# Rewriting an attention-plus-FFN training step in 512-token chunks

## Chip, cores and metric

The kernel runs on one core of a Trainium2 chip. The metric is the device time of one execution in microseconds (us), lower is better. Where a run differs by over 1.5% from the fastest of its kernel, it is called slow and left out of the ratios (medians are of all runs).

## The reference

One transformer layer, forward and backward, S = 2048 tokens, D = 512, 32 heads of 16, a hidden width of 1792, everything in bf16. Attention looks at 8 positions, 2 apart, backwards in time.

```python
x = A_x
h  = x + attention(layernorm(x)) @ wo      # W = 8 shifts, dilation 2, softmax over the 8
h2 = h + gelu(layernorm(h) @ w1 + b1) @ w2 + b2
# outputs: h2 and the gradients of x, wqkv, wo, w1, b1, w2, b2 for a given grad_out
idx = pos[:, None] - 2 * arange(8)[None, :]
logits = einsum("bhsd,bhswd->bhsw", q, k[idx]) * scale      # masked where idx < 0
o = einsum("bhsw,bhswd->bhsd", softmax(logits), v[idx])
```

On the chip a head group of 8 heads x 16 dims fills the 128 partitions. A weight per head has to stand on all 16 partitions of its head: that is the "broadcast". It is a DMA that reads 8 rows (one per head) 16 times each.

## The kernel before

It does each stage for all 2048 tokens: layernorm, QKV, logits, softmax, attention output, FFN, and backward in the reverse order. The parts that matter here:

```python
def bcast_rows_ap(d_tile, row0, col0, width):              # 8 rows, read 16 times
    base = d_tile[row0:row0 + 8, col0:col0 + width]
    rs = base.ap[-2][0]
    return _ap(base, [[0, DH], [rs, 8], [1, width]])

def a4_bcast(g):                                            # attention output, all tokens
    for w in range(W):
        if w % 3 == 1:
            pe_bcast(attnT_sb, g, w, bc, PADL, 0, S, ...)   # by matmul
        else:
            bq = [nc.sync, nc.scalar, nc.gpsimd][(g * W + w) % 3]
            bq.dma_start(out=bc[:], in_=bcast_rows_ap(attnT_d, 32 * w + 8 * g, PADL, S))
...
for g in range(G):
    bcs = bcs_next
    if g + 1 < G:
        bcs_next = a4_bcast(g + 1)                          # the next group's loads
    for w in range(W):
        nc.vector.tensor_tensor(out=prod[:], in0=bcs[w][:],
            in1=vT[:, g, PADL - DIL * w: PADL - DIL * w + S], op=ALU.mult)
        for c in range(NC):
            nc.tensor.matmul(accs[c][:], lhsT=ident[:], rhs=prod[:, c * 512:(c + 1) * 512], ...)
...
for ft in range(FT):                                        # gradient of w2
    transpose_T_to_tm(gT[:, ft:ft + 1, :], g_ft, 1)         # 16 TensorE transposes and evictions
    for t in range(NT):
        nc.tensor.matmul(ps[:], lhsT=g_ft[:, t, :], rhs=gout_bf[:, t, :], ...)
```

The store-and-load trip of the attention weights happens once for all tokens, and loads of the next group run under the products of this one.

## Time and profile before

| | us |
|---|---|
| time, median of 2 | 1067.77 (1067.63 to 1067.9) |
| TensorE / VectorE / ScalarE busy | 809 / 641 / 466 |
| forward ends at | about 384 |
| FFN backward with all gradients and the first attention-backward stages (384 to 812) | 428 |
| attention backward with its loads, LN backward and wqkv gradient (812 to 1065) | 253 |

Read it as a row of stages, each with its own bound; the lines stand in the prediction. No engine is full, so the time is made of the stages' bounds and the gaps between them.

### The profile page before, as it was taken

The numbers are of one execution on the slowest core, as the hardware profiler recorded it, in microseconds if no ns is written. First come the engines' busy times: TensorE is split into PE (matmuls) and PEld (weight loads), VectorE is DVE, ScalarE is ACT, GpSimd is POOL, SyncE is SP. The second block draws the span as 40 slices with busy tenths as digits, with TensorE's granted clock in tenths as the row PEclk, the third lists the DMA queues.
The fourth block names the chain that finished last, engine by engine and source line by source line (L and its number), as shares of the span: only waits on it lengthen the run. The fifth ranks groups of instructions, "written<-read, shape, count | busy, mean of one in ns | idle before, by whom it ended". The sixth has DMA issues, their size and how long they took to land.

```text
span 1065.2 us, 13636 instructions
## 1 busy us (share of the span) xinstructions
PE 809.0 (76%) x4993; PEld 395.8 (37%) x5066; DVE 640.6 (60%) x1317; ACT 465.7 (44%) x860; POOL 40.5 (4%) x70
## 2 busy tenths in 40 slices
PE   0894547874789968998652988744997899959898
PEld 0443312342334434443221444423544333324454
DVE  5309966781886614335994890697002999948822
ACT  3561153662997614445772223201643444432232
POOL 0000010000000000000000000000000011000000
PEclk9995558995999989999995998755998999979899
DMA  4231039317444450004552014201405999731100
GB/s 140 80 161 82 1 100 250 105 34 263 149 163 149 146 175 11 26 25 150 197 194 93 1 43 157 80 1 53 169 30 136 255 237 242 189 135 39 42 30 30
DMA packets 53990, 121.38 MB, mean 114 GB/s; under 512 B 5794, under 2 KB 22948, under 8 KB 53156
## 3 DMA queue, kind: packets, MB, share of 16 engines
q0 software_dynamic: 9968, 42.87, 12.8%
q1 hardware_dynamic: 25142, 41.30, 12.6%
q10 hardware_dynamic: 18814, 36.35, 10.9%
q8 instruction: 39, 0.64, 0.3%
q14 instruction: 27, 0.22, 0.1%
HBM read 81.01 MB, written 39.46 MB: 113 GB/s over the span
## 4 chain that ended last, share of the span: by engine, by line
PE 39%; DVE 19%; issue 18%; DMA 13%; ACT 8%; POOL 1%; SPq 1%; ACTq 0%; POOLq 0%; DVEq 0%
PE ps_gln L687 5%; PE pt L258 4%; PE ps_gw L804 4%; PE ps_gw L613 4%; PE ps_qkv L338 4%; PE ps_gwq L940 4%; DMA bc<-attnT_d 3%; PE ps_ffn L525 2%; DMA wqkv_nat<-in_A_wqkv_dram 2%; DMA bg<-glT_d 2%; DVE qg_row L654 2%; ACT x_row L544 2%; PE ps_h L541 2%; DVE qg_row L652 2%; ACT ch L547 2%
## 5 line engine op out<-in xcount | busy, mean ns | idle before, releaser
L854 DVE TENSOR_TENSOR prodv<-bv,grad_oT 128x1024 bf16<-128x1024 bf16 x64 | 39.6, 681 | 80.5 <-DMA bv<-attnT_d 80.4
L642 PE MATMUL ps_gg<-goutT,w2T 128*128 128x512 bf16 x218 | 52.2, 387 | 21.7 <-ACT gg L645 21.4
L613 PE MATMUL ps_gw<-gout_bf,g_ft 128*128 128x512 bf16 x216 | 63.2, 378 | 0.0
L541 PE MATMUL ps_h<-ln2T,w_bf 128*128 128x512 bf16 x217 | 52.9, 389 | 12.2 <-ACT x_row L544 11.8
L804 PE MATMUL ps_gw<-gh_tm,ln_re 128*128 128x512 bf16 (+1 forms) x248 | 57.3, 356 | 0.4 <-issue 0.2
L770 DVE TENSOR_TENSOR prod<-grad_oT,vT 128x1024 bf16<-128x1024 bf16 x64 | 38.9, 684 | 23.0 <-ACT grad_oT L145 22.3
L525 PE MATMUL ps_ffn<-w_bf,gT 128*128 128x512 bf16 x222 | 51.5, 379 | 0.9 <-ACT x_row L544 0.8
L246 PE MATMUL pt<-ident,ln_bf 128*128 128x128 bf16 x128 | 16.3, 274 | 47.1 <-DVE ln_bf L220 26.5
L438 DVE TENSOR_TENSOR prodo<-bc,qkvT 128x2048 bf16<-128x2048 bf16 x32 | 37.0, 1220 | 23.0 <-DMA bc<-attnT_d 19.2
L687 PE MATMUL ps_gln<-w1T,grad_h1T 128*128 128x512 bf16 x219 | 50.1, 381 | 0.2
L258 PE MATMUL pt<-ident,gT 128*128 128x128 bf16 x224 | 44.8, 217 | 6.1 <-ACT g_ft L145 2.3
L143 DVE COPY g_ft<-pt 128x128 bf16<-128x128 bf16 x112 | 25.1, 224 | 39.6 <-PE pt L258 39.6
L226 ACT ACTIVATE gy<-ps_gln 128x512 f32<-128x512 f32 x32 | 19.1, 597 | 66.7 <-PE ps_gln L687 35.3
L940 PE MATMUL ps_gwq<-gq_tm,ln_re 128*128 128x512 bf16 x185 | 47.7, 391 | 0.4 <-issue 0.2
L145 ACT COPY g_ft<-pt 128x128 bf16<-128x128 bf16 x112 | 29.9, 267 | 35.6 <-PE pt L258 35.6
L869 DVE TENSOR_TENSOR prodq<-bg,qkT 128x1024 bf16<-128x1024 bf16 x64 | 43.5, 680 | 2.6 <-DMA bg<-glT_d 2.6
L441 PE MATMUL acc_o<-prodo,ident 128*128 128x512 bf16 x125 | 37.9, 407 | 9.0 <-DVE prodo L438 8.0
L283 ACT CAST bg<-bp 128x512 bf16<-128x512 f32 (+1 forms) x72 | 28.6, 467 | 37.0 <-DVE prodk L872 15.0
L872 DVE TENSOR_TENSOR prodk<-bg,qkT 128x1024 bf16<-128x1024 bf16 x64 | 43.5, 679 | 0.1
L338 PE MATMUL ps_qkv<-ln1T,wqkv_p 128*128 128x512 bf16 x188 | 43.1, 384 | 0.2
L922 PE MATMUL ps_gln<-wqkvT,gqkvT 128*128 128x512 bf16 x187 | 42.9, 385 | 0.4 <-issue 0.2
L858 PE MATMUL accv<-prodv,ident 128*128 128x512 bf16 x124 | 37.9, 390 | 6.9 <-DVE prodv L854 6.5
(246 smaller groups left out, 1655.8 us busy)
## 6 DMA issues: line engine op xcount, KB each, us to landing
qg_row<-qg_d POOLq DMA_DIRECT2D x14, 512.0 KB, 3.7
sg_d<-sg SPq DMA_DIRECT2D x23, 256.0 KB
bv<-attnT_d SPq DMA_DIRECT2D x22, 256.0 KB
bv<-attnT_d ACTq DMA_DIRECT2D x22, 256.0 KB
bv<-attnT_d POOLq DMA_DIRECT2D x20, 256.0 KB, 6.2
qkvT_d<-qkvT ACTq DMA_DIRECT2D x2, 2080.0 KB
qkT<-qkvT_d POOLq DMA_DIRECT2D x2, 2080.0 KB, 13.6
bg<-glT_d ACTq DMA_DIRECT2D x16, 260.0 KB
```

Source lines behind the costliest of these rows:

```text
L258: nc.tensor.transpose(pt[:, j * P:(j + 1) * P], srcT[:, r, src_off + t * P: src_off + (t + 1) * P], idm_ap)
L338: nc.tensor.matmul(ps[:], lhsT=wqkv_p[:, dc, jt * P:(jt + 1) * P], rhs=ln1T[:, dc, c * 512:(c + 1) * 512], start=(dc == 0), stop=(dc == DC ...
L525: nc.tensor.matmul(ps[:], lhsT=gT[:, ft, t * P:(t + 1) * P], rhs=w2_bf[:, ft, :], start=(ft == 0), stop=False)
L541: nc.tensor.matmul(ps[:], lhsT=w1_bf[:, dc, ft * P:(ft + 1) * P], rhs=ln2T[:, dc, c * 512:(c + 1) * 512], start=(dc == 0), stop=(dc == DC ...
L613: nc.tensor.matmul(ps[:], lhsT=g_ft[:, t, :], rhs=gout_bf[:, t, :], start=(t == 0), stop=(t == NT - 1))
L642: nc.tensor.matmul(ps[:], lhsT=w2T[:, dc, ft * P:(ft + 1) * P], rhs=goutT[:, dc, c * 512:(c + 1) * 512], start=(dc == 0), stop=(dc == DC - 1))
L687: nc.tensor.matmul(ps[:], lhsT=grad_h1T[:, ft, t * P:(t + 1) * P], rhs=w1T[:, ft, :], start=(ft == 0), stop=(ft == FT - 1))
L804: nc.tensor.matmul(ps[:, 0:nf * P], lhsT=ln2_re[:, t, dc * P:(dc + 1) * P], rhs=gh1_tm[:, t, 0:nf * P], start=(t == 0), stop=(t == NT - 1))
L869: nc.vector.tensor_tensor(out=prodq[:, 0:HS], in0=bcg[w][:, 0:HS], in1=kT2[:, g, PADL + s0 - DIL * w: PADL + s0 - DIL * w + HS], op=ALU.mult)
L872: nc.vector.tensor_tensor(out=prodk[:, 0:HS], in0=bcg[w][:, DIL * w: DIL * w + HS], in1=qT2[:, g, PADL + s0 + DIL * w: PADL + s0 + DIL * w ...
L922: nc.tensor.matmul(ps[:], lhsT=gqkvT[:, sel, g, t * P:(t + 1) * P], rhs=wqkvT[:, jt, :], start=(k_ == 0), stop=(k_ == NJ - 1))
L940: nc.tensor.matmul(ps[:], lhsT=ln1_re[:, t, dc * P:(dc + 1) * P], rhs=gq_tm[:, t, :], start=(t == 0), stop=(t == NT - 1))
```

## The change

The intent: keep all engines at work by going through the forward in four chunks of 512 tokens, each from layernorm to FFN; do the product of eight shifts in one VectorE instruction; load broadcasts as 8 KB rows (eight shifts in one row); leave transposes to the DMA engines; and run FFN backward for all chunks, then the attention backward. The core of the diff (the whole rewrites the file):

```diff
-    for w in range(W):
-        nc.vector.tensor_tensor(out=prod[:], in0=bcs[w][:], in1=vT[:, g, PADL - DIL*w : ... + S], op=ALU.mult)
+def bcast(d_tile, g, n):
+    b = d_tile[8 * g:8 * g + 8, :]
+    return _ap(b, [[0, DH], [n, 8], [1, n]])               # n = 8 * 512: one 8 KB row per head
+def back_w(a, n):
+    return _ap(a, [a.ap[0], [-DIL, W], [1, n]])            # eight shifts of one row
+for c in range(NC):                                        # forward, chunk after chunk
+    ...                                                    # layernorm, QKV, logits, softmax
+    aT = to_wh(attn[c], fr, f"a{c}")                       # transpose
+    put_wh(sync, attn_f[c], CH, 0, aT[:, :, :], 0)         # store
+    for g in range(G):
+        sync.dma_start(out=bc[...], in_=bcast(attn_f[c], g, W * CH))      # load
+        nc.vector.tensor_tensor(out=bc[:], in0=bc[:], in1=back_w(v[:, g, PAD:HB], CH), op=ALU.mult)
+        for w in range(W):
+            nc.tensor.matmul(ps[:], lhsT=ident[:], rhs=bc[:, w, :], ...)
+    ...                                                    # wo, layernorm, FFN of the chunk
+for c in range(NC - 1, -1, -1):
+    ffn_bwd(c)
+attn_bwd1(NC - 1)
+with later(LOW):                                           # low priority
-    transpose_T_to_tm(gT[:, ft:ft + 1, :], g_ft, 1)
+    for ft in range(FT):
+        for c in range(NC):
+            sync.dma_start_transpose(out=gtm[:, c, :, :], in_=g_d[c][ft * P:(ft + 1) * P, :])
+        ...                                                # 16 matmuls, store
+with later(LOW):
+    tail_weights()                                         # gradients of w1 and wo
+for c in range(NC - 1, -1, -1):
+    attn_bwd2(c, ...)
+    attn_bwd1(c - 1)
```

## The prediction

> **What bounds the kernel now.** I read the head of the page first (busy time per engine), then the slices, then a table of stages that I cut at the places where the lines of the TensorE timeline change, then the costliest groups.
>
> ```profile
> PE 809.0 (76%) x4993; PEld 395.8 (37%) x5066; DVE 640.6 (60%) x1317; ACT 465.7 (44%) x860; POOL 40.5 (4%) x70
> PEclk9995558995999989999995998755998999979899
> DMA  4231039317444450004552014201405999731100
> ```
>
> No engine is full: the kernel is a row of stages, each with its own limit. The stage table (columns: stretch, length, then busy time and count of PE, PEld, DVE, ACT, POOL, then clock, DMA share, GB/s) names them:
>
> ```profile
> 39.00:79.00 40.00, 39.82 (x193) 18.25 (x193) 1.29 (x2) 28.03 (x48) 0.00 (x0) 1.00 0.32 129
> 79.00:148.00 69.00, 30.68 (x546) 21.59 (x544) 66.11 (x151) 11.78 (x23) 0.00 (x0) 0.54 0.08 32
> 148.00:208.00 60.00, 48.49 (x175) 18.06 (x179) 37.05 (x32) 32.37 (x61) 3.77 (x7) 0.85 0.77 193
> 261.00:308.00 47.00, 35.13 (x147) 14.84 (x149) 34.96 (x67) 44.99 (x58) 0.00 (x0) 0.96 0.38 140
> ...
> 394.00:484.00 90.00, 82.50 (x582) 44.42 (x592) 35.42 (x128) 40.01 (x126) 0.00 (x0) 0.98 0.06 20
> 484.00:570.00 86.00, 50.38 (x214) 21.43 (x217) 75.24 (x71) 55.88 (x71) 7.43 (x14) 0.91 0.52 173
> ...
> 742.00:812.00 70.00, 66.86 (x469) 38.32 (x475) 0.00 (x0) 38.49 (x79) 0.00 (x0) 0.97 0.26 99
> 812.00:930.00 118.00, 105.57 (x416) 39.94 (x423) 107.52 (x178) 50.20 (x116) 16.12 (x31) 0.96 0.93 234
> ```
>
> QKV (39 to 79) is bound by TensorE, logits and softmax (79 to 148) by VectorE, FFN forward (261 to 366) by ScalarE, FFN backward (484 to 570) by VectorE, the weight gradients (394 to 484, 742 to 812) by TensorE with transposes and their evictions, attention backward (812 to 930) by VectorE and the DMA engines together. The unit costs:
>
> ```profile
> L687 PE MATMUL ps_gln<-w1T,grad_h1T 128*128 128x512 bf16 x219 | 50.1, 381 | 0.2
> L438 DVE TENSOR_TENSOR prodo<-bc,qkvT 128x2048 bf16<-128x2048 bf16 x32 | 37.0, 1220 | 23.0 <-DMA bc<-attnT_d 19.2
> L854 DVE TENSOR_TENSOR prodv<-bv,grad_oT 128x1024 bf16<-128x1024 bf16 x64 | 39.6, 681 | 80.5 <-DMA bv<-attnT_d 80.4
> L258 PE MATMUL pt<-ident,gT 128*128 128x128 bf16 x224 | 44.8, 217 | 6.1 <-ACT g_ft L145 2.3 <-DVE g_ft L143 1.6 <-DVE w2T L143 0.4
> ```
>
> A matmul of 512 columns costs 50.1/219 = 0.23 us of union (0.22 in the long runs of the chain), not its 381 ns of latency. Products cost 681 ns at 1024 and 1220 at 2048, so a fixed 0.14 us and 0.53 us per 1024: at 4096, 2.25 us. Finally, DMA alone, in a stretch of broadcast loads and in one of plain loads:
>
> ```profile
> 824.00:832.00 8.00, 5.33 (x17) 1.86 (x16) 5.10 (x9) 2.60 (x7) 0.53 (x1) 0.79 1.06 263
> 250.00:258.00 8.00, 4.67 (x40) 4.15 (x39) 2.77 (x4) 3.04 (x3) 0.00 (x0) 0.50 1.02 399
> ```
>
> With all 16 DMA engines busy, broadcast rows move 263 GB/s and plain loads 399.
>
> **What the Trainium skill says.** "Vector Engine (DVE) Microarchitecture Reference", section 5.1 Performance modes: a tensor_tensor of 16-bit operands with inner step 1 yields two results per cycle, also where one input reads a row again with step 0. The trace agrees on the rate (0.53 us per 1024); that the new patterns (step 0 over eight shifts, or minus 2 with overlap) keep it, no run shows yet. "DMA: Bandwidth & Descriptors", section Latency and other measured facts: a DMA transpose has about 261 GB/s; the kernel before has none. The same page, section Bandwidth: 425 GB/s for a large load; the plain 399 agrees, the broadcast 263 does not. "TensorE: Matmul & The Clock Gate", section What's actually happening: after an idle window of some 3.4 us the clock halves; the trace agrees with 0.54 to 0.55 in the stages where TensorE waits for VectorE.
>
> **The change, part by part.** I also read the order of instructions per engine in the changed program, and that decides most of what follows.
>
> *Counts.* TensorE loses 880 of its 1,200 transposes, which DMA transposes replace, and 120 broadcast matmuls. What stays is some 2,690 of 512 columns (64 of 256 counted half): 590 us at 0.22, 1,024 of 8 columns at 0.05 = 51, 320 transposes at 0.07 = 22; about 665 us. VectorE: the 96 fused products are 96 x 2.25 = 216 us (before 320 x 0.68 + 32 x 1.22 = 257). Evictions go to ScalarE (about -70). Layernorm backward loses one pass (32 x 2.45 against 3.17 us, -23). But the GELU derivative is recomputed in backward and its reduction reads PSUM in 56 pieces. Single durations add to some 565 us; for the kernel before the same addition gives some 700 (641 with overlap). ScalarE: about 390 us, before 466. So the engine sums fall; the question is the waits.
>
> *Forward, per chunk.* The TensorE order finishes a chunk's FFN before the next chunk's QKV; only the next layernorm and its transposes overlap. So each chunk is a serial chain. (a) QKV 48 x 0.22 = 10.5 with products under it, then logits: 17. (b) Softmax in two halves of 512: about 3.6 of VectorE each, plus exp and its table load: 9.5. (c) Transpose, eviction, store (2.2), four broadcasts of 1 MB at 260 GB/s (2.4 + 4 x 4.0), last product, eight matmuls, eviction: 27.5. (d) Output projection, layernorm, transposes: 13.5. (e) FFN: per f pair 2 x 0.65 + 1.07 + 1.07 = 3.44 of ScalarE, times 7 = 24, table and transposes 3.3, second matmul's tail: 35. Sum 102.5; four make 410, and 17 to start: 427. Before, the forward ends at some 384. The forward loses about 40: broadcasts that lay across 60 us in all are now exposed in every chunk.
>
> *FFN backward.* Per f pair 0.43 + 3 x 0.68 + 0.43 = 2.9 us of VectorE and two PSUM reductions of 0.80; seven make 31.5. Layernorm backward 4 x 2.45 = 9.8. Chunk 41.3, four 165. TensorE needs 112 x 0.22 = 25 per chunk, so VectorE is the bound. To 592.
>
> *Weight gradients.* They have low priority, but in the TensorE order they stand in one block behind the first chunk's products: 224 + 256 + 64 matmuls. With two buffers for the transposed g and four transposes each I take 4.3 us per f, so 60, then 52, 14, and 10 for the products ahead: 136, to 728. Before these and their transposes were 90 + 70 and a part of 42.
>
> *Attention backward.* Rest of the first chunk 45. Then per chunk: output gradient and four products 15, softmax backward 6, transpose, store and first broadcast 11 (under it the four v products), four heads' groups at 6.3 (load 6.4, two products 4.6, two pairs of buffers) 25, QKV backward 10.5: 67. Three make 201; to 974. Here most of a DMA queue's waits are for buffers.
>
> *Tail.* The last transposed loads stand behind the last output stores: 12, then 192 x 0.22 = 42, and 3: 57. Sum **1031 us**.
>
> **Rivals.** First: the fused instruction hides what I count serially, and rows of 8 KB load faster than 260 GB/s. For it: 64 products take 38.9 us of union in the logits-like stage, 0.61 each, though one lasts 0.68; plain loads reach 399. At 350 to 400 GB/s each broadcast loses 1.0 to 1.4 us of 4.0, about 5 us per chunk forward and 6 backward, 45 in all; VectorE's overlap is worth 15 to 25. Against it: 4 KB rows (229 to 265 GB/s in the stage at 160) were no faster than 2 KB rows. Then 960 to 990. Second: DMA transposes are slow. 26.7 MB pass through them on one queue; at 261 GB/s that is 102 us, mostly hidden, at 100 GB/s 267 us, and the gradient block and the tail pay: 1080 to 1150. Nothing in the profile speaks on it. Third: the overlapping patterns lose the two-per-cycle rate: 96 x 2.1 = 205 us on the path, 1200. Fourth: TensorE stays warm and the chunks overlap as intended, near its sum: 800 to 850. Against it the order read above, where QKV follows the whole FFN.
>
> **Range and chances.** My sum is 1031. I lean below it because the first rival is likely in part, and because so many choices of buffers and queues look fitted to a chip: 995 us, 80% in 900 to 1065. The border for faster by 2% is 1046, for slower 1089. The sum lies below the first, with an error of some 50: faster 0.77, same 0.14, slower 0.09.
>
> **What would show it.** Right: fused products of 2.2 to 2.3 us; four forward chunks of about 100 us with a DMA wait of 15 to 20 before the products that read broadcasts; VectorE over 90% busy through 160 us of FFN backward; a dense TensorE block of gradients while VectorE idles; attention backward chunks of some 67. Wrong: broadcasts over 320 GB/s, gradient matmuls waiting for transposes at over 5 us per f, products of over 4 us, or forward chunks of under 85.

## The result

The changed kernel takes 1160.11 us (1156.15 and 1164.06), against 1067.77: 1.086 times, 95% interval 1.078 to 1.095. It is slower, and the prediction was wrong in direction. A ratio is the mean time of one kernel's fast runs over that of the other's fast runs of the same rounds, so it is not quite the ratio of the medians.

The head of the page of the changed kernel, then its slices of granted TensorE clock and DMA share:

```profile
PE 748.9 (65%) x4066; PEld 328.0 (28%) x4066; DVE 539.5 (47%) x790; ACT 372.0 (32%) x529; POOL 270.6 (23%) x392
...
PEclk9678876895798687887999799599996786967879
DMA  7265427444452789856543844996739668577293
```

Three engines have less to do than before (TensorE by 60 us, VectorE by 101, ScalarE by 94) and the span is 89 us longer. What grew is waiting, GpSimd (271 us busy where 41 were; its queue now carries 126 of the 186 MB, and no run varied that) and DMA: 186 MB move where 121 did. The stage table of the changed kernel (stretch, length, then busy time and count of PE, PEld, DVE, ACT, POOL, then clock, DMA share, GB/s):

```profile
21.60:140.00 118.40, 72.49 (x452) 34.57 (x452) 46.31 (x72) 50.33 (x68) 34.40 (x44) 0.77 0.51 148
140.00:247.00 107.00, 64.35 (x386) 28.87 (x385) 45.98 (x65) 44.70 (x62) 30.06 (x39) 0.78 0.49 137
351.00:465.00 114.00, 63.00 (x362) 26.79 (x360) 45.62 (x58) 45.10 (x60) 31.87 (x45) 0.76 0.78 191
465.00:620.00 155.00, 118.29 (x477) 48.69 (x477) 139.00 (x320) 81.37 (x102) 59.67 (x84) 0.89 0.55 169
620.00:744.00 124.00, 70.02 (x413) 26.86 (x412) 28.52 (x28) 15.86 (x26) 12.81 (x18) 0.86 0.67 157
744.00:820.00 76.00, 70.31 (x347) 33.73 (x345) 0.29 (x1) 12.61 (x23) 3.21 (x6) 0.98 0.81 165
857.00:933.00 76.00, 49.44 (x311) 22.58 (x309) 50.28 (x43) 17.44 (x31) 16.83 (x29) 0.75 0.70 174
1087.00:1152.00 65.00, 45.20 (x192) 19.37 (x192) 3.54 (x7) 9.20 (x16) 3.03 (x4) 0.84 0.71 158
```

In a forward chunk (140 to 247) no engine is busy more than some 60% of the time: that is a chain, one engine waiting for the other. FFN backward (465 to 620) is what was hoped for, VectorE at 90%. Between 620 and 820 TensorE works through the weight gradients while VectorE is busy for 14% of the time.

| stage | predicted | measured | before |
|---|---|---|---|
| forward ends at | 427 | 465 | 384 |
| FFN backward | 165 | 155 | |
| gradients, to the end of wo's | 136 | about 200 | |
| (all from forward's end to there) | 301 | 355 | about 361 |
| attention backward: rest of chunk 3, then three chunks | 45, 67 each | 37, 77 each | |
| tail with the wqkv gradient | 57 | 65 | |

The "before" of the fourth row adds 384 to 675 and 742 to 812. The table says where to look: against the kernel before, the forward lost about 81 us, which is nearly all of the loss; the gradients lost nothing but their hoped-for gain. (The table cuts the forward at 465; its last matmul ended at 468, and ends of the forward below are taken in that way.)

Inside chunk 1, the chain from the softmax to the attention output. First the SyncE queue (store, then loads), then VectorE's products (start, length, what; in brackets the idle time ahead and what ended it):

```profile
166.08 1.18 SPq L294 DMA_DIRECT2D attn_f<-aTa  x2
173.40 2.51 SPq L305 DMA_DIRECT2D bc<-attn_f  x4
```

```profile
180.80 2.29 DVE L306 TENSOR_TENSOR bc<-bc,v 128x4096 bf16<-128x4096 bf16 x1 [16.68 <-DMA bc<-attn_f]
185.60 2.29 DVE L306 TENSOR_TENSOR bc<-bc,v 128x4096 bf16<-128x4096 bf16 x1 [2.50 <-DMA bc<-attn_f]
190.40 2.29 DVE L306 TENSOR_TENSOR bc<-bc,v 128x4096 bf16<-128x4096 bf16 x1 [2.51 <-DMA bc<-attn_f]
195.15 2.29 DVE L306 TENSOR_TENSOR bc<-bc,v 128x4096 bf16<-128x4096 bf16 x1 [2.45 <-DMA bc<-attn_f]
```

The fused product takes 2.29 us, as predicted. But 7.3 us pass from the store's issue to the loads' issue, 7.4 more until the first megabyte has landed, and each further one takes 4.8. For the 15 us from the store to the first product, no engine computes.

The store itself is worth a look. The changed kernel's table of DMA issues has stores of the same 128 KB landing in a median of 1.7 to 2.9 us (the outputs, oT_d), but the attention weights and their gradients, whose pattern in `put_wh` (`[[n, 4], [W * n, 32], [1, 512]]`) has four outer steps, in 5.1 to 5.7 (attn_b, gl_b). From the store to the loads (166 to 173.4) the DMA share was only 0.37, at 73 GB/s. Whether the four steps are the reason no run tested; the 4 KB pieces stored beside them take 5.0 to 5.4 too, and gq_d, of another pattern, 4.8.

### The profile page after: what moved, and what is told of

It is laid out like the page before. It is cut to its first block, busy times and chain, and to the rows that moved or that the text cites. A ratio compares the mean times of both kernels' runs of the same rounds, so it can differ in the third digit from the quotient of the medians.

```text
span 1154.4 us, 10992 instructions
## 1 busy us (share of the span) xinstructions
PE 748.9 (65%) x4066; PEld 328.0 (28%) x4066; DVE 539.5 (47%) x790; ACT 372.0 (32%) x529; POOL 270.6 (23%) x392
## 2 busy tenths in 40 slices
DMA packets 166516, 186.18 MB, mean 161 GB/s; under 512 B 124925, under 2 KB 138110, under 8 KB 160318
## 4 chain that ended last, share of the span: by engine, by line
issue 24%; DVE 16%; PE 12%; DMA 10%; ACT 5%; POOL 3%; SPq 1%; POOLq 0%; ACTq 0%; DVEq 0%
PE psq L653 3%; PE psa L525 2%; DMA bg<-gl_b 2%; DMA bv<-attn_b 2%; DVE gh L449 2%; DVE bp L489 2%; DMA bc<-attn_f 2%; DVE by L441 1%; PE ps L351 1%; SPq L648 1%; ACT by L435 1%; DVE by L439 1%; ACT bu L438 1%; POOL gq_d L530 1%; DVE lua L420 1%
## 5 line engine op out<-in xcount | busy, mean ns | idle before, releaser
L541 DVE TENSOR_TENSOR bh<-bg,bk 128x4096 bf16<-128x4096 bf16 x16 | 36.7, 2292 | 194.9 <-DMA bg<-gl_b 194.9
L309 PE MATMUL pso<-bc,ident 128*128 128x512 bf16 x128 | 45.0, 516 | 92.6 <-DVE bc L306 92.6
L447 PE MATMUL psg<-goutT,w2T 128*128 128x512 bf16 x224 | 63.7, 441 | 34.4 <-DVE gb1p L449 29.3
L306 DVE TENSOR_TENSOR bc<-bc,v 128x4096 bf16<-128x4096 bf16 x16 | 36.7, 2292 | 93.1 <-DMA bc<-attn_f 93.1
L578 PE MATMUL psw<-gout,gtm 128*128 128x512 bf16 x224 | 57.4, 389 | 30.3 <-DMA gtm<-g_d 30.1
L525 PEld LDWEIGHTS <-ident 128*128 128x128 bf16 x384 | 41.8, 113 | 122.5 <-issue 40.0
L333 PE MATMUL psf<-ln2T,w 128*128 128x512 bf16 x224 | 60.7, 429 | 20.3 <-ACT u L335 18.1
L612 PE MATMUL psw<-h1tm,ln2a 128*128 128x512 bf16 (+1 forms) x256 | 50.5, 359 | 25.7 <-DMA h1tm<-gh_d 25.7
L351 PE MATMUL ps<-w,g 128*128 128x512 bf16 x224 | 55.6, 397 | 11.3 <-ACT u L335 9.7
L653 PE MATMUL psq<-gqt,ln1a 128*128 128x512 bf16 x192 | 45.2, 398 | 18.9 <-DMA ln1a<-ln_d 17.6
L459 PE MATMUL psx<-w1T,gh 128*128 128x512 bf16 x224 | 51.5, 390 | 2.3 <-DVE gb1p L449 2.3
L309 PEld LDWEIGHTS <-ident 128*128 128x128 bf16 x128 | 14.1, 121 | 121.4 <-DVE bc L306 102.1
L251 PE MATMUL psq<-ln1T,wqkv 128*128 128x512 bf16 x192 | 44.5, 394 | 0.7 <-ACT ln1T L224 0.7
## 6 DMA issues: line engine op xcount, KB each, us to landing
bv<-attn_b POOLq DMA_DIRECT2D x16, 1056.0 KB, 10.6
```

The source lines that it names most:

```text
L251: nc.tensor.matmul(ps[:], lhsT=wqkv[:, dc, jt * P:(jt + 1) * P], rhs=ln1T[:, dc, :], start=(dc == 0), stop=(dc == DC - 1))
L309: nc.tensor.matmul(ps[:], lhsT=ident[:], rhs=bc[:, w, :], start=(w == 0), stop=(w == W - 1))
L333: nc.tensor.matmul(ps[:], lhsT=w1[:, dc, ft * P:(ft + 1) * P], rhs=ln2T[:, dc, :], start=(dc == 0), stop=(dc == DC - 1))
L351: nc.tensor.matmul(ps[:], lhsT=gs[ft // 2][:, ft % 2, j * P:(j + 1) * P], rhs=w2[:, ft, :], start=(ft == 0), stop=False)
L447: nc.tensor.matmul(ps[:], lhsT=w2T[:, dc, ft * P:(ft + 1) * P], rhs=gT[:, dc, :], start=(dc == 0), stop=(dc == DC - 1))
L459: nc.tensor.matmul(ps[:], lhsT=gh1[ft // 2][:, ft % 2, j * P:(j + 1) * P], rhs=w1T[:, ft, :], start=(ft == 0), stop=(ft == FT - 1))
```

## The experiments

Eighteen kernels ran. All numbers "of the whole" are ratios to the kernel before; times are medians. *A* is the theory that the loss is the serial chain of waits in each chunk, *B* that it is the DMA transposes, *C* that it is the rate of the broadcast loads.

### The reference on the chip

> The changed kernel without an edit, so that the other kernels of this call have their reference on the same chip: 1150 to 1165 us, 1.08 to 1.09 times the kernel before. No theory differs here.

Measured: 1162.9 us, 1.080 (1.075 to 1.084), from two fast runs, 1151 and 1156; the other two were slow, 1169 and 1171. Together with the first result, 1.080 to 1.086 is where an edit without effect should end.

### B: plain loads in place of the DMA transposes

```diff
-sync.dma_start_transpose(out=gtm[:, c, :, :], in_=g_d[c][ft * P:(ft + 1) * P, :])
+sync.dma_start(out=gtm[:, c, :, :], in_=g_d[c][ft * P:(ft + 1) * P, :].rearrange("p (a b) -> p a b", b=P))
 # likewise for w2T, w1T, goutT, h1tm, otm and gqt
```

> Wrong result on purpose: every DMA transpose becomes a plain load of the same bytes from the same tensor to the same tile. If the transposes are the main cause of the loss (four issues of 1.2 us per f pair on one queue, 5.8 us per f in the gradient block where the matmuls need 3.6), the gradient block goes from 190 us to about 145, the tail from 66 to 57, and the last FFN chunk of the forward loses some of its 11 us: 60 to 75 us in all, so about 1090. If the loss is in the forward chain of waits, the forward still ends at 450 to 465 and the whole gains at most 30 us. I lean to 55 us in all, of which the forward has 5 to 10.

Measured: 1108.32 us, 1.038 (1.035 to 1.042). Against 1.080 that is 0.042 of 1068, so 44 us. The forward's end moved from 468 to 462, the block of gradients from 205 to 167 us (625 to 830 against 617 to 784), the tail hardly. The issue of one transpose and of one plain load of the same 128 KB, from the two traces (minimum/median/maximum ns):

```profile
L575 SPq DMA_TRANSPOSE gtm<-g_d x56: 1188/1212/7991, 448.5 to 714.9; - x56
```

```profile
L575 SPq DMA_DIRECT2D gtm<-g_d x56: 319/426/5862, 416.6 to 676.6; - x56
```

Four transposes per f hold the queue for 4 x 1.21 = 4.9 us, and with the store behind them 5.8 us per f, where 16 matmuls need 3.5. The bytes are the same in both kernels, the packets are not (changed kernel, then plain loads):

```profile
DMA packets 166516, 186.18 MB, mean 161 GB/s; under 512 B 124925, under 2 KB 138110, under 8 KB 160318
```

```profile
DMA packets 80340, 186.18 MB, mean 168 GB/s; under 512 B 10845, under 2 KB 51422, under 8 KB 74142
```

With the transposes there are some 114,000 more packets of under 512 bytes. B holds for 38 us of the gradient block, a little less than I leaned to, and leaves the forward nearly as it is.

### B: one transpose per f

```diff
-g_d = [dram.tile([F, CH], BF16, ...) for c in range(NC)]
+g_d = dram.tile([F, S], BF16, name="g_d")
-for c in range(NC):
-    sync.dma_start_transpose(out=gtm[:, c, :, :], in_=g_d[c][ft * P:(ft + 1) * P, :])
+sync.dma_start_transpose(out=gtm[:].rearrange("p c t q -> p (c t) q"), in_=g_d[ft * P:(ft + 1) * P, :])
```

> Correct result: g goes to one tensor of 1792 x 2048, so each f of the w2 gradient needs one DMA transpose of 128 x 2048 and not four of 128 x 512. If the cost of a transpose is its issue (1.2 us each), 42 issues less give up to 50 us of queue time, psw2 goes from 5.8 to about 4 us per f, and 20 to 25 us are gained. If the cost goes by bytes, an issue of four times the bytes lasts four times as long, and nothing changes (within 4 us).

Measured: 1145.34 us, 1.071 (1.068 to 1.075), so 9 us off, at the limit of what is read here. One issue of four times the bytes takes 1.9 to 2.6 us, where four took 4.9: the issue has a fixed part. The w2 gradient, with the waits ahead of it, goes from 89 to 74 us: about 4.2 us per f once it runs, after a first transpose that alone took 12.6 us beside the broadcast loads. Less than half of the expected gain reached the end.

### A, first attempt: attention of the next chunk between the pieces of the FFN

```diff
+def step(gen, n): ...                       # emits the next n pieces of a stage
+for c in range(NC):
+    ffn, att = fwd_ffn(c), fwd_attn(c + 1)
+    for na, nf in ((0, 1), (1, 1), (1, 1), (1, 4), (1, 1), (1, 1), (1, 1), (1, 1), (1, 0)):
+        step(att, na); step(ffn, nf)
```

> Correct result: the same work, but in the forward the attention of chunk c+1 is written into the program in pieces between the pieces of the FFN of chunk c, so that TensorE, ScalarE and VectorE have FFN work while softmax, store and broadcast loads of the next chunk run. If the forward's loss is the serial chain (A), the forward ends at 375 to 410 rather than 465 and the whole gains 55 to 90 us, to about 1075 to 1105. If the chain is not the cause (the loads take the time whatever lies beside them, or ScalarE is the limit), it gains under 25.

Measured: 1148.31 us, 1.074 (1.071 to 1.077), 6 to 13 us off: neither theory's number. The forward ended at 446 (22 us earlier), but the chunks still took 96 to 112: the softmax stretched from 8 to 16 us (its exp alternates with the FFN's sigmoid on ScalarE, with four table loads of 1.28 us per chunk), and the FFN's pieces also stood between the heads. So the inserted work helped where the chain waited, and cost where it did not.

### A, without building anything better: loads that wait for nothing

```diff
-sync.dma_start(out=bc[...], in_=bcast(attn_f[c], g, W * CH))
+sync.dma_start(out=bc[...], in_=stand_in(g))      # same shape, from an input: wrong result on purpose
```

> Wrong result on purpose: the 16 broadcast loads of the forward read the same number of bytes in the same shape from an input tensor, so that they do not wait for softmax, transpose and store; all other work stays. If the loss of the forward is the serial wait from softmax through store to the landed load (A), each of four chunks loses 16 to 22 us, the forward ends at 385 to 405 rather than 465 and the whole falls to 1085 to 1105. If the loads cost their own bandwidth wherever they stand, the forward gains under 25 us.

Measured: 1114.84 us, 1.034 of the fast runs (1.028 to 1.039; two of four were slow, and the profile is of a slow one, so only its stages are used); the median lies above the range expected. A chunk took 85 to 87 us and not 104: 18 us each, as A says. But the forward ended at 418, 50 us earlier and not 72, for in the last chunk the FFN stood still. ScalarE and SyncE there:

```profile
380.19 0.69 ACT L339 ACTIVATE u<-psf,b1c 128x512 bf16<-128x512 f32 x1 [28.49 <-DMA x_d<-u]
```

```profile
334.47 41.49 SPq L402 DMA_TRANSPOSE w2T<-in_B_w_dram  x1
```

The transpose of w2 for the backward, free to start earlier, holds its queue for 41 us (13.9 in the changed kernel, 7 in plan_b) while the DMA engines are busy throughout, and the FFN's own stores (x_d) wait behind. So some 20 us of the gain were lost there, by this reading to B's transposes; no run tested it apart.

### A, a correct kernel that fills only the wait

```diff
-    for na, nf in ((0, 1), (1, 1), (1, 1), (1, 4), (1, 1), ...):
+    for na, nf in ((3, 0), (0, 7), (1, 1), (1, 1), (1, 1), (1, 1)):   # FFN pairs while the loads travel
```

> Correct result. The interleaved kernel stretched softmax (8 to 16 us) and the heads (17 to 21) and gained 22 us at the forward's end, and 4 to 14 in all. Here the FFN is put where the chain waits alone: QKV, logits, softmax and the issue of the loads of chunk c+1 stand ahead of the seven pairs of FFN c, its four heads between the four output tiles. If the wait for the store and the loads (about 22 us per chunk) can be filled, a chunk takes 80 to 88 and not 105, and the forward ends at 400 to 420; whole 1100 to 1125. If the transfers of the FFN and the loads get in each other's way, the forward ends at 440 or later and the whole gains under 20.

Measured: 1121.69 us, 1.049 (1.045 to 1.053), so 33 to 40 us off. The two steady stretches took 87 and 85 us, in the table by stretch (where 140 to 247 and 247 to 351 took 107 and 104):

```profile
198.00:285.00 87.00, 62.27 (x389) 28.73 (x388) 44.77 (x65) 47.22 (x64) 30.64 (x38) 0.85 0.51 159
285.00:370.00 85.00, 61.33 (x375) 27.59 (x374) 41.43 (x52) 46.00 (x63) 27.33 (x38) 0.84 0.62 185
```

The forward ended at 421. A is confirmed, with a correct result: the same work, in an order that puts the FFN into the wait, takes back some 47 us of the forward's 81; 33 to 40 of them reach the end.

### C: is the rate of the broadcast loads due to shared rows?

```diff
-return _ap(b, [[0, DH], [n, 8], [1, n]])
+return _ap(b, [[0, 4], [n, 32], [1, n]])          # spread_rows: 32 rows, 4 times each
+return _ap(b, [[n, DH], [n, 8], [1, n]])          # staggered: group i reads rows i to i+7
```

> Wrong result on purpose: the broadcast loads move the same bytes in the same 8 KB rows, but read 32 different rows 4 times each rather than 8 rows 16 times each. If the 215 GB/s of these loads comes from many engines reading the same few rows, a load of 1 MB falls from 4.8 us to about 3 (350 GB/s), and as 16 forward and 32 backward loads stand largely on the path, the time falls by 40 to 70 us. If the rate comes from the shape of the rows or from the queue, the loads stay at 4.6 to 4.9 us and the time within 5 us of the changed kernel.

Measured: 1439.2 us, 1.348. It failed as a test and taught something else: a load took 10.3 us. Between two heads, at 78 to 86 us:

```profile
78.00:86.00 8.00, 1.47 (x4) 0.28 (x3) 2.29 (x1) 0.59 (x1) 0.54 (x1) 0.50 0.30 118
```

Four outer steps keep 0.30 of the DMA engines at work. So the rows had to be spread with 16 outer steps kept:

> Wrong result on purpose: the broadcast loads keep their split over 16 groups of 8 partitions and their 8 KB rows, but group i reads rows i to i+7, so that at one moment the 16 groups read 16 different rows and not the same row. The spread rows failed as a test because four outer steps used four or five engines (share 0.26 to 0.30, 118 GB/s, so 24.6 GB/s per engine against 13.7 before). If the same row read by 16 engines at once costs the rate, a load falls from 4.8 to about 2.7 to 3.2 us, and the time by 40 to 75 us. If sharing of rows does not matter, nothing changes (within 5 us).

Measured: 1163.98 us, 1.091 (1.086 to 1.095); steps between the heads' products 4.65 to 4.80 us. No effect: engines that read the same row at one moment are not the cause.

> Correct result: each broadcast load is two loads of 4 KB rows. If the 8 KB rows lower the rate (before had 240 to 268 GB/s with 2 and 4 KB rows), the pair takes 4.1 us and not 4.8 and some 20 us are gained; also the first half lands earlier but the product waits for both. If row length does not matter, the time is within 5 us or some us longer for 48 more issues.

```diff
-sync.dma_start(out=bc[...], in_=bcast(attn_f[c], g, W * CH))
+for hw in range(2):                               # two loads of 4 KB rows, likewise in the backward
+    sync.dma_start(out=bc[:, 4*hw:4*hw+4, :]..., in_=bcast(attn_f[c], g, W * CH, 4*hw*CH, 4*CH))
```

Measured: 1145.6 us, 1.073 (1.069 to 1.076), 8 to 15 us off; steps of about 4.4 us (4.28 to 4.53 in chunk 1) where 4.8 were. Row length has a small part.

Then the other end, 128 different rows, still behind the store:

```diff
-in_=bcast(attn_f[c], g, W * CH)
+in_=attn_f[c][:, :]                                # plain_rows: 128 rows of 8 KB (96 filled once at the start)
+in_=_ap(attn_f[c][0:1, :], [[4*W*CH, DH], [W*CH, 8], [1, W*CH]])   # rows_twice: rows 4i to 4i+7
```

> Wrong result on purpose: the forward's broadcast loads read 128 different rows of 8 KB (32 of them just stored, the rest filled at the start) in place of 8 rows 16 times; bytes, row length, queue and dependency stay. If reading a row again is what makes these loads slow, 1 MB takes 2.6 to 3.2 us (before's plain loads had 399 GB/s) and the four heads 13 rather than 17 us: some 16 to 25 us off the forward. If it is the row length, the destination or the queue, the step between the heads' products stays at 4.6 to 4.8 us and the time within 6 us of the changed kernel (the fill costs some us in the first chunk).

Measured: 1124.37 us, 1.051 (1.046 to 1.056), 31 to 38 us off, though the fill starts the first chunk 10 us later (31.4 against 21.6); steps of 2.5 us, now VectorE's own. The forward ended at 438, 30 us earlier, more than the 16 to 25 expected. I took this for proof that reading again is slow. The next two runs refuted that:

> Wrong result on purpose, on top of plain_rows: group i reads rows 4i to 4i+7, so 68 rows of 8 KB are read once or twice each. If the loss grows with the times that a row is read, a step between heads stays at about 2.5 us (VectorE-bound) and the time is that of plain_rows, 1120 to 1128. If any second reading of a row is slow, 3.5 to 4.7 us per step, and 1135 to 1160.

Measured: 1169.69 us, 1.095; steps of 4.5 to 4.7, though a row is read once or twice. The time lies above both ranges expected, by the fill's 10 us in the first chunk.

> Correct result: the rows of attention weights and their gradients stand 40 KB apart in memory (every fifth row is used), the loads still read 8 rows 16 times each. If the loss comes from all reads falling on one stretch of 64 KB, a load takes 2.5 to 3.5 us and the whole falls by 40 to 80 us, to 1080 to 1120. If it comes from reading the same bytes again, 4.6 to 4.9 us stay, and the time is within 6 us of the changed kernel.

```diff
-return _ap(b, [[0, DH], [n, 8], [1, n]])
+return _ap(b, [[0, DH], [FAR * n, 8], [1, n]])    # FAR = 5, stores likewise; correct result
```

Measured: 1159.06 us, 1.085; steps of 4.7 to 4.8 again. Not the stretch of memory either. What was left is the form of the pattern:

```diff
+forms = {0: 4 * [[[9*n, 16], [n, 8]]],            # 128 different rows, 16 groups of 8
+         1: 4 * [[[0, 128]]],                     # one row, 128 times, one list
+         2: 4 * [[[n, 8], [0, 16]]],              # 8 rows, 8 groups of 16
+         3: [[[n, 64], [0, 2]], [[n, 32], [0, 4]], [[n, 16], [0, 8]], [[n, 128]]]}
```

> Wrong result on purpose, on top of plain_rows. Chunk 0 reads rows 9i+j, 128 different rows as 16 groups of 8. Chunk 1 reads one row 128 times, as one list. Chunk 2 reads 8 rows, each 16 times in a row (8 groups of 16). Chunk 3: per head 64 rows twice, 32 rows four times, 16 rows eight times, 128 rows once. If the form (16 groups of 8) sets the rate, chunk 0 has steps of 4.6 to 4.8 us though no row is read again, and chunk 1 steps of 2.5 though one row is read 128 times. If reading again sets it, chunk 0 has 2.5 and chunk 1 4.7 or more. Chunk 2 shows either 2.5 or, if its outer 8 keeps only 8 engines busy, 4.8 to 5.2 at a DMA share of about 0.5.

Measured: 1167.87 us, 1.093. VectorE's products, two of chunk 0, two of chunk 1, two of chunk 2, then chunk 3:

```profile
77.72 2.29 DVE L317 TENSOR_TENSOR bc<-bc,v 128x4096 bf16<-128x4096 bf16 x1 [2.38 <-DMA bc<-attn_f]
82.40 2.29 DVE L317 TENSOR_TENSOR bc<-bc,v 128x4096 bf16<-128x4096 bf16 x1 [2.38 <-DMA bc<-attn_f]
...
189.78 2.29 DVE L317 TENSOR_TENSOR bc<-bc,v 128x4096 bf16<-128x4096 bf16 x1 [0.22 <-DMA bc<-attn_f]
192.28 2.29 DVE L317 TENSOR_TENSOR bc<-bc,v 128x4096 bf16<-128x4096 bf16 x1 [0.21 <-DMA bc<-attn_f]
...
297.32 2.29 DVE L317 TENSOR_TENSOR bc<-bc,v 128x4096 bf16<-128x4096 bf16 x1 [6.88 <-DMA bc<-attn_f]
306.50 2.29 DVE L317 TENSOR_TENSOR bc<-bc,v 128x4096 bf16<-128x4096 bf16 x1 [6.88 <-DMA bc<-attn_f]
...
407.21 2.29 DVE L317 TENSOR_TENSOR bc<-bc,v 128x4096 bf16<-128x4096 bf16 x1 [0.83 <-DMA bc<-attn_f]
411.77 4.59 DVE L317 TENSOR_TENSOR bc<-bc,v 128x4096 bf16<-128x4096 bf16 x2 [2.26 <-DMA bc<-attn_f]
```

and the stretches of chunk 0, 2 and 1 in the table by stretch:

```profile
70.00:90.00 20.00, 9.77 (x28) 3.08 (x29) 9.17 (x4) 1.76 (x3) 1.61 (x3) 0.65 0.87 195
283.00:315.00 32.00, 10.42 (x24) 3.09 (x24) 6.88 (x3) 1.75 (x3) 1.61 (x3) 0.59 0.52 122
187.00:195.00 8.00, 5.38 (x17) 2.12 (x18) 7.12 (x4) 0.58 (x1) 0.54 (x1) 0.61 0.87 366
```

128 different rows as 16 groups of 8: 4.7 us per MB. One row 128 times as one list: 2.5 or less. 8 groups of 16: 9.2 at half the DMA engines (I had expected 4.8 to 5.2). 32 groups of 4: 3.1 or less; 16 groups of 8: 4.6. At the same DMA share of 0.87, the list moves 366 GB/s and the groups 195. So C is true in its size (a broadcast load costs 4.7 us where the same bytes as a list take 2.5 or less) and its first cause was wrong: it is neither the rereading nor the rows' place, it is the form of 16 groups of 8. Why that form halves the rate of each engine stays open; which partitions of the tile each DMA engine then writes was not looked at. A correct broadcast in another form was not built. And C is mostly not a difference between the two kernels: `bcast_rows_ap` of the kernel before has the same 16 groups of 8, and moved 248 GB/s in its forward (155 to 192 us, DMA share 1.03) where the changed kernel moves 216 (176 to 195, share 1.00).

### Do the fused products pay?

```diff
-nc.vector.tensor_tensor(out=pr[:], in0=over_w(q[:, g, :], CH), in1=back_w(k[:, g, PAD:HB], CH), op=ALU.mult)
+for w in range(W):
+    nc.vector.tensor_tensor(out=pr[:, w, :], in0=q[:, g, :], in1=k[:, g, PAD-DIL*w : HB-DIL*w], op=ALU.mult)
```

> Correct result: each product over eight shifts becomes eight products of 512. By the sizes of before (0.14 us fixed and 0.53 per 1024) each of 96 costs 8 x 0.41 = 3.3 us and not 2.29, 95 us of VectorE in all. Where loads of 4.8 us are the limit (broadcast products) the rest hides; the products of logits and the pairs beside one load (4.6 us) do not: I expect 30 to 60 us more. If VectorE lies wholly in the shadow of the loads, under 15.

Measured: 1152.34 us, 1.077 (1.073 to 1.081), not slower at all. The groups of two of the products:

```profile
L308 DVE TENSOR_TENSOR bc<-bc,v 128x512 bf16<-128x512 bf16 x128 | 44.4, 421 | 87.0 <-DMA bc<-attn_f 87.0
L261 DVE TENSOR_TENSOR pr<-q,k 128x512 bf16<-128x512 bf16 x128 | 43.4, 417 | 54.0 <-ACT q L253 54.0
```

128 products of 512 take 44.4 us of VectorE where 16 fused ones took 36.7, because they overlap (0.35 each, though one lasts 0.42); over the six groups that is, by the difference of these two, an estimated 46 us of VectorE. None of it reached the end: it lay in waits for the loads and for ScalarE's copies. My own expectation of 30 to 60 us was wrong, for I counted the products beside one load as bare. The fused form is as fast per element as hoped, and worth nothing in the time of this kernel.

### The gradient block: in one piece or spread

```diff
 # in the FFN backward of each chunk, after pairs 1, 3, 5 (and 6)
+if f2 in W2_AT[c]: step(gw2, 1)                   # one of 14 tiles of the w2 gradient
 # in the attention backward, after a head's sums
+if g in WT_AT[c]: step(tw, 1)                     # one of 20 tiles of the w1 and wo gradients
-with later(LOW): tail_weights()
```

> Correct result: the changed kernel with the same operations, but the w2 gradient's 14 tiles stand between the pairs of the FFN backward, and the 20 tiles of the w1 and wo gradients between the heads of the attention backward. If the block of 190 us is exposed only because it stands in one piece behind one queue of transposes, FFN backward goes from 152 to 155-170, the block from 190 to about 55, the three chunks from 77 to 85-95: 1035 to 1080. If the transposes' DMA time then slows the loads it lies beside, 1100 or more.

Measured: 1068.74 us median, fast runs 1062.86 and 1052.14, slow ones 1116.66 and 1074.63; 0.990 (0.984 to 0.996) of the kernel before. Against 1.080 to 1.086 that is some 100 us by the two fast runs, and 85 by the means of all four runs: the largest effect of all. In the trace (of the slowest run) the FFN backward holds the whole w2 gradient and takes 164 us with TensorE at 92%:

```profile
469.00:633.00 164.00, 151.06 (x693) 67.04 (x693) 139.20 (x319) 86.80 (x115) 57.03 (x80) 0.99 0.80 201
633.00:802.00 169.00, 72.64 (x391) 30.63 (x390) 50.32 (x44) 20.13 (x35) 22.66 (x36) 0.71 1.07 141
```

The second line is the price: where the first chunk's broadcasts, the loads for the gradients and the transposes meet, the DMA engines are full for 169 us. The scatter of the runs may come with that; it is not shown.

### The attention backward: is it the order of one queue?

```diff
+for g in range(G):                                # ahead of the softmax backward
+    pq.dma_start(out=bc[...], in_=bcast(attn_b[c], g, W * HB))
```

> Correct result: the four v loads of each attention-backward chunk are written ahead of the softmax backward, so the fourth is no longer behind the stores of its result on the same queue. If that order cost the 7.8 us per chunk, a chunk falls from 77 to about 70 and the whole by 20 to 28 us. If the DMA engines are the limit there (eight loads of 4.8 us are 38 us, and the stores then wait behind the fourth load), a chunk stays at 75 to 77 and the whole gains under 8.

Measured: 1170.26 us, 1.092 (1.085 to 1.099): nothing gained. Counted from the start of a chunk, the v sums end at 34 us in place of 41, but the next ones start at 41.7 in place of 42.3, for the stores of the softmax gradient and the loads that read them now come behind the fourth v load. A chunk stays at 76 to 77 us. The trace had shown a 7.8 us wait for one load; the wait was real and moving it changed where it is paid.

### Together

> Correct result: plan_b and spread_grads with one transpose per f (merged_g) and half rows. If the parts add up (60 + 100 + 10 + 10), about 985 to 1020, faster than the kernel before. If the DMA engines become the limit, 1040 to 1080.

combo1 is plan_b, spread_grads, merged_g and half_rows. Measured: 1034.7 us, 0.966 (0.963 to 0.970), correct: faster than both kernels, between the two ranges expected, and gaining less than its parts add up to (33 + 96 + 9 + 8 off 1155 would be about 1010). Its first attention-backward stretch took 136 us at a DMA share of 0.99.

> Correct result: combo1 with the v loads hoisted, the tiles of the w1 and wo gradients spread over the last three chunks only, and ln2a loaded by the other queue. combo1's first attention-backward chunk took 134 us against 45 alone, as its loads lay beside those for the gradients. If that pile-up was avoidable, that chunk falls to 70-95, the next ones rise by 3 to 8 each, and the time to 990 to 1015. If DMA time is conserved, the pile-up moves to the next chunk and the time is 1025 to 1040.

```diff
-WT_AT = {3: (4, 5, 6, 7), 2: range(8), 1: range(8), 0: ()}
+WT_AT = {3: (), 2: range(8), 1: range(8), 0: (0, 1, 2, 3)}        # later gradients; v loads hoisted
-pq.dma_start(out=ln2a[:, c, :, :], in_=tm(ln2_d[c][:]))
+sync.dma_start(out=ln2a[:, c, :, :], in_=tm(ln2_d[c][:]))
```

Measured: 1010.14 us median, fast runs 1004.26 and 998.55, 0.936 (0.932 to 0.940), correct. That stretch is 98 us now, the next ones 95 and 87 (in a profiled run of the slow kind, 1014 us). It is the fastest version here.

## Why the prediction was wrong

Its picture of the kernel was right: TensorE's order chunk after chunk, a serial forward, VectorE as the bound of FFN backward, gradients in one block. What failed are the sizes of waits in it. The stages are 122 us longer than its sum: the gradient block 64, the forward 38, the three attention-backward chunks 30, the tail 8; FFN backward was 10 shorter and the rest of the first attention chunk 8. Its own sign of being wrong, gradient matmuls waiting for transposes at over 5 us per f, came true (5.8). By its steps:

- *Forward.* Step (c), store to output, was put at 27.5 us. In chunk 1 it took 37.5 from the end of the softmax (164.1) to the last copy (201.6). Its mis-sized terms, 10 us in all: the store at 2.2, measured 7.3; the first load at 6.4, measured 7.4; three further loads at 4.0, measured 4.8; the last eight matmuls at 1.8, measured 3.4 at a granted clock of 0.53. The other steps were sized a little high ((a) 17 against 16.5, (b) 9.5 against 7.4, (d) 13.5 against 10.6, (e) 35 against 35), so an undisturbed chunk came to 104 to 107 for 102.5. The rest of the 38 us are the start (21.6 for 17) and two things left out: the weights' transposes at the end of chunk 0 (118 us), and the FFN of chunk 3 (46 us), which waits for its stores behind the transposes for the backward (without these, in plain_loads, the forward ended 6 us earlier).
- *The second rival was not priced.* "DMA transposes are slow" stood at 1080 to 1150 with "nothing in the profile speaks on it", and got at most the 0.09 of "slower". plain_loads measures it at 44 us. The 261 GB/s that it cites is given by "DMA: Bandwidth & Descriptors" for a non-contiguous middle dimension, and 350 to 400 for the contiguous case; no run here measures either. And its 26.7 MB leave out the 2.1 MB of goutT. "4.3 us per f, so 60" measured 5.8 and 82; waits of about 20 us for the h1 transposes were not in the sum. The block was 64 us longer than predicted, the largest miss; spread_grads shows that standing in one piece is what exposes it.
- *Attention backward.* "Transpose, store and first broadcast 11 (under it the four v products)" assumed that the v loads are there; the v sums took 19 us, with a wait of 7.8 us for the fourth load. Loads of 4.8 us where 4.0 were put explain 6.4 of the 10 us by size (eight per chunk, an estimate from the two durations); the one other order of that queue that was tried (hoist_bv) did not take the rest away, so it stays open.
- *Tail, FFN backward, rest of the first chunk.* 65 for 57, 155 for 165, 37 for 45: they cancel but for 10 us, by luck.
- *Leaning below the sum.* The sum was 1031; 995 was chosen because faster loads and overlap seemed likely. Loads were slower, and VectorE's time turned out to be worth nothing off the path (unfused). The large errors had one sign: a wait that the sum does not list makes the time longer. (A slip without effect: the third rival's 96 x 2.1 is 202, not 205.)

Against the kernel before: the forward pays the trip of the attention weights four times and in the open, where the old one paid it once and loaded under its products. early_loads and plan_b show this to be worth about 50 of the forward's 81 us. The remainder (chunk 0's weight transposes, the last chunk's stores) is argued from the traces and not shown; plain_rows (31 to 38 us) does not measure it, since the kernel before reads its broadcasts in the same form. That the gradients cost no more than before is not a success: spread, they take 85 to 100 us less.

## What to carry to other kernels

Less work on the three busiest engines says little if the order in which engines take it is a chain: ask for each chunk what runs while its store and its loads travel, and write other work into just that place. Put weight gradients where another engine is the bound, not in a block at the end: low priority did not spread it here, for the built program had it in one piece. And when a sum of stages is the estimate, the unlisted waits push it upward; a rival on which the profile is silent deserves a real share of the chances.

## What the Trainium skill lacked or had wrong

- "DMA: Bandwidth & Descriptors", section Why a DMA increments its semaphore by 16 and not by 1, derives the number of engines from the slowest dimension. The runs agree for few groups (4 outer steps: share 0.30, 118 GB/s; 8: 0.52, 122 GB/s). It doesn't say that 16 groups of 8 rows, with all engines at work, move half of what a list of 128 rows moves: 195 against 366 GB/s at a share of 0.87, 4.7 against at most 2.5 us per MB.
- "Advanced Engine Details and Errata", section X-Bar Transpose (TRN2): "TRN2 transpose DMAs are as fast as regular DMAs". Here the issue of a transpose of 128 KB takes 1.21 us where a plain load takes 0.43, one of 1.8 MB held its queue for 7 to 41 us (13.9 in the changed kernel) beside other transfers, and plain loads in place of all transposes moved the same bytes in 80,340 packets for 166,516 and made the kernel 44 us shorter.
- "DMA: Bandwidth & Descriptors" times single DMAs, but no page has a time for a store in four outer steps with a load that waits for it: 7.3 us here from issue to issue, for two stores of 128 KB of attention weights beside four other stores.
